# A segment-recurrent attention kernel: the left rows are loaded again one segment earlier, and softmax, copies and small loads change places

## The chip, the cores and the metric

One NeuronCore of a Trainium2 chip runs the whole kernel; the other cores of the chip are not used. The metric is the device time of one execution in microseconds (us), as the median over several runs. The engines are called by the short names of the profile: PE is TensorE, DVE is VectorE, ACT is ScalarE, POOL is GpSimd and SP is SyncE. SP computes nothing here; it issues the large weight transfers.

## The reference: what is computed

The result is `x + A(xn) + B(xn)` for 2048 rows of 1024 numbers, where xn is the layer norm of x.

A is an attention with a memory that is carried from segment to segment. The 2048 rows are cut into 64 segments of 32. In front of each segment stand 8 memory rows, which are the first 8 output rows of the segment before. So each segment depends on the one before it, and the 64 run one after the other:

```python
for s in range(n_seg):
    h = jnp.concatenate([mem, xs], axis=1)              # 8 + 32 rows
    q, k, v = (jnp.einsum('btd,dhe->bhte', h, W) for W in (Wq, Wk, Wv))   # 32 heads of 128
    scores = jnp.where(mask, jnp.einsum('bhqe,bhke->bhqk', q, k) * scale, -1e9)
    o = jnp.einsum('bhqk,bhke->bhqe', softmax(scores), v)
    o = jnp.einsum('bhte,hed->btd', o, Wo)
    mem = o[:, :8, :]
    outs.append(o[:, 8:, :])
```

Wq, Wk, Wv and Wo have 1024 x 4096 numbers each, 32 MB in bf16 together. B picks the two rows with the largest `xn @ w_r`, sends them through a gated feed-forward layer of width 3584 and adds the result to these two rows.

## The kernel before

**The weights.** The four matrices are cut into 64 granules of 512 KB: granules 0 to 47 belong to q, k and v (six phases of eight chunks), 48 to 63 to the output projection. 42 granules stay in on-chip memory for the whole run. The other 22 are streamed again in each segment through six slots of 512 KB (pool `wstream`, tile `g`). `fetch` (L202) issues the next transfer on SP's queue as soon as a slot is free, and a slot is free when PE has used it (`used`, L333). Of three streamed granules one half is held in PSUM (`HELD`) and is copied by ACT (L220), which saves that half of the transfer.

**The rows of a segment.** PE works with 32 rows at a time, the 8 memory rows and the first 24 rows of the segment; the transposed operand is `ST`. The last 8 rows of a segment, its *left* rows, don't feed the next memory, and are therefore computed together for four segments (a group G): 4 x 8 = 32 left rows in `STL`. With j = s % 4, their q is computed in the segment j = 2 of the group before, their k in j = 3, their v in j = 0 of their own group. q and k go through an ACT copy `QS` (L446) and a store to DRAM (`qkl_d`, L450), and each segment loads its own part back as `QKL` (`load_qkl`, L340). The attention outputs of the left rows are gathered in `OTL` over the group, and the output projection of the left rows is done in segment j = 3 and after it, into the PSUM tile `WL`.

**The order.** Nothing is planned by a scheduler: the program is written out in order (`manual_schedule`), and each engine runs its own instructions in the order in which they were emitted. In a segment, six phases (`PHASES`: q, k of the first 16 heads, q, k of the second 16, then v of both) run over eight chunks each (L572 to L616). `hook(p, kc, fn)` puts a function behind chunk kc of phase p; when the place is reached, `fn` emits its instructions for all engines (L598). `ends` is a list of functions that is run when a phase is over (L615). `todo` holds what a segment leaves for the next one's hooks. After the six phases come 16 steps w of the output projection into `WO`, with the last parts of the attention at w = 4 and 8.

**The places that the change touches.**

- `load_left` (L248) loads 4 x 8 left rows by four transfers of 16 KB from POOL's queue into a tile with the tag "vm", of which there is one. The same buffer serves the tiles `VM`, `QS` and `OB` in turn.
- After the last segment of a group, `left_load` at (1,3) of the next segment (j = 0) loads the left rows of the finished group again, `left_norm` at (2,4) normalises them (PE, DVE L259 to L262, POOL L263), and `left_store` at (3,4) adds them to `WL` (`residual`, PE, L302), copies the sum to `OL` (ACT, L688) and stores it by four POOL transfers (L691). Seven of the ten resident granules of WL's projection are worked off in the hooks (0,1) to (1,5) of the same segment. In the last group these three functions run in the tail of the program, L721 to L723.
- `scores(half)` (L464), at (2,5) and (4,5): PE computes q k, DVE finds the maximum and subtracts it (L479, L480), and `softmax(half)` is put into `ends`: ACT's exponential (L484), DVE's sum, reciprocal, two multiplications into `PM` and `PL` and two transposes (L485 to L500), POOL's memset of `PL` for the first half, and last the load of the next segment's QKL (L340).
- `transposes` (L427) and `transposes_left` (L439): when a phase is over, ACT copies `PSm` to `XB` (L602), and one or more chunks later PE transposes it into the single PSUM tile of the tag "t", from where DVE copies it to `QT` or `KT` (L435, L437). The left rows do the same with `XBl` and `QS`.
- `left_keys(half)` (L459), at (0,1) and (3,0): POOL copies the left rows' keys from `QKL` into `KT` (L462), which `scores` needs.

The tags "xb" (two buffers) and "pm" (one buffer) hold `XB`, `XBl`, `PT2` and `OL`, and `XNR` and `PM`, in this order.

Of the kernel before, what the change touches and what calls it, by code (L numbers as in the profile page):

```python
# [8 lines left out]
BF16 = mybir.dt.bfloat16  # L9
# [18 lines left out]
def kernel(  # L28
# [16 lines left out]
    nc = tc.nc  # L45
# [199 lines left out]
        queue.dma_start(out=X[0:4 * XM, :], in_=x2[s * SEG:s * SEG + XM, :].rearrange("r (g c) -> (r g) c", g=4))  # L245
        return X

    def load_left(G, queue=nc.gpsimd):  # L248
        X = one.tile([P, 512], BF16, tag="vm", name="XL")
        for sl in range(4):  # L250
            r0 = (4 * G + sl) * SEG + XM
            queue.dma_start(out=X[32 * sl:32 * sl + 32, 0:256],  # L252
                                in_=x2[r0:r0 + XL, :].rearrange("r (g c) -> (r g) c", g=4))
        return X

# [136 lines left out]
    for s in range(NSEG):  # L392
# [46 lines left out]
        def transposes_left(mat, half, XB, g):  # L439
            PTq = psT.tile([P, 4, 4, 32], BF16, tag="t", name="PTq")  # L440
            for il in range(4):
                nc.tensor.transpose(out=PTq[:, il, :, :].rearrange("p j r -> p (j r)"), in_=XB[:, il * P:(il + 1) * P],
                                    identity=IDENT[:, :])
            QS = one.tile([P, 4, 16, XL], BF16, tag="vm", name="QS") if half == 0 and s > 0 else \
                two.tile([P, 4, 16, XL], BF16, tag="xb", name="QS")
            nc.scalar.copy(out=QS.rearrange("p s h r -> p h s r"),  # L446
                           in_=PTq.rearrange("p i j (s r) -> p (i j) s r", s=4))

            def save():
                nc.gpsimd.dma_start(out=qkl_d[g][mat, half].rearrange("p s c -> p (s c)"),  # L450
                                    in_=QS.rearrange("p s h r -> p (s h r)"))

            if s == 0:
                nc.gpsimd.tensor_copy(out=first_left(half)[:, mat, :].rearrange("p (h r) -> p h r", r=XL), in_=QS[:, 0, :, :])
                save()
            else:
                hook(2 * half + mat + 1, {(0, 0): 5, (1, 0): 4, (0, 1): 7, (1, 1): 4}[mat, half], save)

        def left_keys(half):  # L459
            if s > 0:  # L460
# [3 lines left out]
        def scores(half):  # L464
            q, k = QT[half], KT[half]
            for il in range(4):
                for jq in range(4):
                    hh = 4 * il + jq
                    nc.tensor.matmul(SPS[32 * jq:32 * jq + 32, il, 0, :], lhsT=q[:, hh, :], rhs=k[:, hh, :],
                                     start=(il == 0), stop=True, tile_position=(0, 32 * jq), skip_group_check=True)  # L470
                    nc.tensor.matmul(SPS[32 * jq:32 * jq + XL, il, 1, :], lhsT=QKL[half][:, 0, hh * XL:(hh + 1) * XL],
                                     rhs=k[:, hh, :], start=False, stop=True, tile_position=(0, 32 * jq),
                                     skip_group_check=True)
            nc.tensor.matmul(SPS.rearrange("p i a k -> p i (a k)"), lhsT=IDENT[:, :],  # L474
                             rhs=MASK[:, :].unsqueeze(1).to_broadcast([P, 4, 2 * NK]),
                             start=False, stop=True, skip_group_check=True)
            S8 = SPS.rearrange("p i a k -> p (i a) k")
            NM = one.tile([P, 8], F32, tag="nm", name="NM")
            nc.vector.tensor_reduce(out=NM[:, :], in_=S8, axis=AX.X, op=ALU.max, negate=True)  # L479
            nc.vector.tensor_tensor(out=S8, in0=S8, in1=NM[:, :].unsqueeze(2).to_broadcast([P, 8, NK]), op=ALU.add)  # L480
            ends.append(lambda: softmax(half, S8, NM))

        def softmax(half, S8, DN):
            nc.scalar.activation(out=S8, in_=S8, func=ACTF.Exp, scale=SCALE)  # L484
            nc.vector.tensor_reduce(out=DN[:, :], in_=S8, axis=AX.X, op=ALU.add)  # L485
            nc.vector.reciprocal(out=DN[:, :], in_=DN[:, :])
            PM = one.tile([P, 8, 32], BF16, tag="pm", name="PM")
            PLt = PL.rearrange("p i a k -> p (i a) k")
            if half == 0:
                jp = (j + 3) % 4  # L490
                nc.gpsimd.memset(PLt[:, :, XL * jp:XL * (jp + 1)], 0.0)
            dnb = DN[:, :].unsqueeze(2)
            nc.vector.tensor_tensor(out=PM[:, :, :], in0=S8[:, :, 0:32], in1=dnb.to_broadcast([P, 8, 32]), op=ALU.mult)
            nc.vector.tensor_tensor(out=PLt[:, :, XL * j:XL * (j + 1)], in0=S8[:, :, 32:NK],
                                    in1=dnb.to_broadcast([P, 8, XL]), op=ALU.mult)
            PT2 = one.tile([P, 2, 4, 64], BF16, tag="pt", name="PT2") if half == 0 else \
                two.tile([P, 2, 4, 64], BF16, tag="xb", name="PT2")
            PTm, PTl = PT2[:, 0], PT2[:, 1]
            nc.vector.transpose(out=PTm.rearrange("p i q -> p (i q)"), in_=PM.rearrange("p b k -> p (b k)"))
            nc.vector.transpose(out=PTl.rearrange("p i q -> p (i q)"), in_=PLt.rearrange("p b k -> p (b k)"))  # L500
            PTs[half] = (PTm, PTl)
            if s == 0 and half == 1:
                QKLs.append(load_qkl(1, 0))
                QKLs.append(load_qkl(1, 1))
            elif 0 < s < NSEG - 1:
                QKLs.append(load_qkl(s + 1, half))

        def new_otl():
# [53 lines left out]
        if s == NSEG - 1:  # L562
            hook(0, 6, routed_d)
            hook(2, 2, routed_e)
        hook(2, 5, lambda: scores(0))
        hook(4, 5, lambda: scores(1))
        if j == 0:
            hook(5, 1, new_otl)
        hook(5, 3, lambda: attend(0, 0))
# [2 lines left out]
        for p, (mat, half) in enumerate(PHASES):  # L572
# [27 lines left out]
            if mat < 2:  # L600
                XB = two.tile([P, 512], BF16, tag="xb", name="XB")
                nc.scalar.copy(out=XB[:, :], in_=PSm[:, :])  # L602
                hooks.setdefault((p + 1, (2, 1, 3, 1)[p]), []).insert(0, lambda m=mat, h=half, b=XB: transposes(m, h, b))
                if PSl is not None:
                    XBl = two.tile([P, 512], BF16, tag="xb", name="XBl")
                    (nc.scalar.copy if p == 2 else nc.vector.tensor_copy)(out=XBl[:, :], in_=PSl[:, :])  # L606
                    hooks.setdefault((p + 1, (4, 3, 6, 3)[p]), []).insert(
                        0, lambda m=mat, h=half, b=XBl, g=left[mat]: transposes_left(m, h, b, g))
            else:
                c0 = half * 512  # L610
                if PSl is not None:
                    nc.scalar.copy(out=VL[:, c0:c0 + 512], in_=PSl[:, :])
                VM[half] = one.tile([P, 512], BF16, tag="vm", name="VM")
                nc.scalar.copy(out=VM[half][:, :], in_=PSm[:, :])  # L614
# [29 lines left out]
        for w in range(16):  # L644
            if w == 4:
                attend(1, 0)
            if w == 8:
                attend(1, 1)
            Gv = granule(48 + w)
            project(WO, w, Gv, lhs_main, w == 15)  # L650
            if j == 3:
                if 48 + w in streamed:
                    project(WL, w, Gv, lhs_left, first=not started)
                    started = True
                else:
                    deferred.append((w, Gv))
            used(48 + w)
# [15 lines left out]
        if j == 3:  # L673
            spots = [(0, 1), (0, 3), (0, 5), (0, 7), (1, 1), (1, 3), (1, 5), (1, 7), (2, 1), (2, 3)]
            for pk, (w, Gv) in zip(spots, deferred[3:]):
                todo.append((pk, lambda w=w, Gv=Gv, WL=WL, lhs=lhs_left: project(WL, w, Gv, lhs)))
            end = {}

            def left_load(G=G, end=end):
                end["x"] = load_left(G)  # L680

            def left_norm(G=G, end=end):
                norm_left(G, end["x"])

            def left_store(G=G, WL=WL, end=end):
                residual(WL, end["x"][:, 0:256], P, False)
                OL = two.tile([P, 512], BF16, tag="xb", name="OL")
                nc.scalar.copy(out=OL[:, 0:256], in_=WL[:, 0:256])  # L688
                o4 = out2[4 * G * SEG:4 * (G + 1) * SEG, :].rearrange("(s r) d -> s r d", s=4)
                for g in range(4):  # L690
                    nc.gpsimd.dma_start(out=o4[:, XM:SEG, 256 * g:256 * (g + 1)], in_=OL[32 * g:32 * (g + 1), 0:256])  # L691

            todo += [((1, 3), left_load), ((2, 4), left_norm), ((3, 4), left_store)]
        if s + 1 < NSEG:
            ST = nxt["st"]


    lc.close()
    for pk, fn in todo[:-3]:
        fn()  # L700
    fin = ctx.enter_context(tc.tile_pool(name="fin", bufs=1, reuse_waits="tile"))
    XSP = fin.tile([P, KC, 32], BF16, name="XSP")
# [4 lines left out]
    for w in range(2):  # L707
# [3 lines left out]
        for kc in range(KC):  # L711
            for fh in range(2):
# [6 lines left out]
                                     start=(kc == 0), stop=(kc == KC - 1), tile_position=(0, 32 * q))  # L719
                fetch()  # L720
                n += 1  # L721
                if n in (1, 10, 15):
                    todo[-3 + (1, 10, 15).index(n)][1]()  # L723
    OUTR = fin.tile([2, D], BF16, name="OUTR")
    for c in range(2):
        nc.gpsimd.dma_start(out=OUTR[c:c + 1, :], in_=out2[bass.ds(vals[c], 1), :])
# [68 lines left out]
```

## Time and profile before

Three runs took 2198.06, 2203.74 and 2211.63 us; the median is 2203.74 us. The profiled execution has a span of 2208.3 us.

| engine | busy us | share of the span | instructions |
|---|---|---|---|
| PE | 1764.8 | 80% | 36202 |
| PE weight load | 900.5 | 41% | 36202 |
| DVE | 752.3 | 34% | 2328 |
| ACT | 705.9 | 32% | 1738 |
| POOL | 543.0 | 25% | 1030 |

| queue | packets | MB | share of 16 DMA engines |
|---|---|---|---|
| q1, SP's weights | 267652 | 732.79 | 90.8% |
| q0, POOL's transfers | 23520 | 26.06 | 3.6% |

The profile page gives 768.74 MB in all and a mean of 348 GB/s. How to read what follows: a *wait* is idle time of an engine before an instruction, put down to what came last before the instruction could run. The *chain* goes back from the last instruction of the program, at each step to what released it. The *timeline* gives start, duration, engine, line, operation and names, and in brackets the idle time before it and its releaser. A *window* is a stretch of time with the busy time and the number of instructions of each engine in it. The first segment takes 115.7 us, since it also loads the resident weights and computes the statistics of all rows; the other 63 segments take about 29 to 39 us each; and the tail with the feed-forward layer of B takes the rest.

### The profile page before, as it was taken

The numbers are of one execution on the slowest core, as the hardware profiler recorded it, in microseconds if no ns is written. First come the engines' busy times: TensorE is split into PE (matmuls) and PEld (weight loads), VectorE is DVE, ScalarE is ACT, GpSimd is POOL, SyncE is SP. The second block draws the span as 40 slices with busy tenths as digits, with TensorE's granted clock in tenths as the row PEclk, the third lists the DMA queues.
The fourth block names the chain that finished last, engine by engine and source line by source line (L and its number), as shares of the span: only waits on it lengthen the run. The fifth ranks groups of instructions, "written<-read, shape, count | busy, mean of one in ns | idle before, by whom it ended". The sixth has DMA issues, their size and how long they took to land.

```text
span 2208.3 us, 82817 instructions
## 1 busy us (share of the span) xinstructions
PE 1764.8 (80%) x36202; PEld 900.5 (41%) x36202; DVE 752.3 (34%) x2328; ACT 705.9 (32%) x1738; POOL 543.0 (25%) x1030
## 2 busy tenths in 40 slices
PE   2578788878888888888888788888888878888775
PEld 1234344444434444443444444444444434444341
DVE  5533332333333233333323333332333333233330
ACT  4533233323233333333333233332333323233320
POOL 4322213222121322222122222222222222222111
PEclk8689999999989999999999999998999999899986
DMA  9899999989999999999999999999999999899989
GB/s 358 332 363 365 339 354 331 368 300 346 350 323 371 352 354 347 346 360 330 365 338 384 313 345 377 336 376 318 365 351 348 375 322 367 305 379 352 360 310 347
DMA packets 294351, 768.74 MB, mean 348 GB/s; under 512 B 37458, under 2 KB 42770, under 8 KB 293988
## 3 DMA queue, kind: packets, MB, share of 16 engines
q1 hardware_dynamic: 267652, 732.79, 90.8%
q0 software_dynamic: 23520, 26.06, 3.6%
q8 instruction: 283, 4.64, 0.8%
q10 hardware_dynamic: 2816, 4.59, 0.6%
q14 instruction: 80, 0.66, 0.1%
HBM read 750.68 MB, written 12.59 MB: 346 GB/s over the span
## 4 chain that ended last, share of the span: by engine, by line
PE 42%; DMA 38%; DVE 7%; issue 6%; ACT 4%; POOL 3%; ACTq 0%; DVEq 0%; POOLq 0%; SPq 0%
PE PSm L581 21%; DMA g<-in_A_Wo_dram 13%; DMA g<-in_A_Wq_dram 9%; PE PSl L594 7%; PE OA L632 4%; DMA XL<-in_A_x_dram 4%; DMA qkl_d<-QS 3%; DMA g<-in_A_Wv_dram 2%; PE PTq L430 2%; PE WL L632 2%; DMA XP<-in_A_x_dram 1%; ACT XB L602 1%; POOL XL L252 1%; PE SPS L474 1%; DMA out_dram<-OB 1%
## 5 line engine op out<-in xcount | busy, mean ns | idle before, releaser
L581 PE MATMUL PSm<-wres,ST 128*32 128x512 bf16 x8192 | 774.6, 409 | 20.4 <-DVE ST L309 17.9
L581 PE MATMUL PSm<-g,ST 128*32 128x512 bf16 x4096 | 428.8, 407 | 44.2 <-DMA g<-in_A_Wq_dram 26.9
L581 PEld LDWEIGHTS <-ST 128*32 128x32 bf16 x12288 | 301.7, 99 | 373.7 <-issue 139.9
L632 PEld LDWEIGHTS <-OT 128*32 128x32 bf16 x8192 | 215.4, 97 | 145.3 <-issue 133.9
L220 ACT COPY g<-HELD 128x1024 bf16<-128x1024 bf16 x189 | 191.2, 1012 | 259.4 <-PE PSm L581 169.8
L632 PE MATMUL OA<-wres,OT 128*32 128x256 bf16 x5120 | 235.2, 277 | 26.2 <-issue 20.9
L602 ACT CAST XB<-PSm 128x512 bf16<-128x512 f32 x256 | 149.9, 585 | 317.0 <-PE PSm L581 316.9
L632 PE MATMUL OA<-g,OT 128*32 128x256 bf16 x3072 | 159.0, 278 | 74.0 <-DMA g<-in_A_Wo_dram 70.1
L594 PE MATMUL PSl<-wres,STL 128*32 128x512 bf16 x2048 | 205.9, 404 | 9.0 <-DVE XBl L606 8.3
L340 POOL DMA_DIRECT2D QKL<-qkl_d x126 | 91.9, 729 | 363.9 <-PE SPS L474 175.7
L665 POOL DMA_DIRECT2D out_dram<-OB x256 | 129.5, 513 | 66.2 <-DVE OB L661 35.5
L535 ACT CAST OT<-OA 128x128 bf16<-128x128 f32 x256 | 67.9, 265 | 227.7 <-PE OP L529 226.3
L430 PE MATMUL PTq<-IDENT,XB 128*128 128x128 bf16 x1024 | 106.3, 229 | 43.0 <-ACT XB L602 28.1
L462 POOL COPY KT<-QKL 128x128 bf16<-128x128 bf16 x128 | 38.2, 299 | 375.9 <-PE OA L632 363.1
L479 DVE TENSOR_REDUCE NM<-SPS 128x8 f32<-128x320 f32 x128 | 62.8, 490 | 199.0 <-PE SPS L474 199.0
L430 PEld LDWEIGHTS <-XB 128*128 128x128 bf16 x1024 | 63.2, 100 | 157.1 <-ACT XB L602 115.1
L594 PEld LDWEIGHTS <-STL 128*32 128x32 bf16 x3072 | 87.3, 101 | 91.8 <-issue 35.1
L614 ACT CAST VM<-PSm 128x512 bf16<-128x512 f32 x128 | 77.4, 604 | 140.6 <-PE PSm L581 140.6
L535 DVE CAST OT<-OP 128x128 bf16<-128x128 f32 x128 | 37.3, 291 | 224.4 <-PE OP L529 224.4
L437 DVE COPY KT<-PTq 128x512 bf16<-128x512 bf16 x128 | 54.2, 424 | 164.3 <-PE PTq L430 162.8
L594 PE MATMUL PSl<-g,STL 128*32 128x512 bf16 x1024 | 105.6, 403 | 2.9 <-ACT XBl L606 2.8
L527 PEld LDWEIGHTS <-VM 32*128 32x128 bf16 x2048 | 62.7, 91 | 90.1 <-issue 54.2
(140 smaller groups left out, 2303.2 us busy)
## 6 DMA issues: line engine op xcount, KB each, us to landing
g<-in_A_Wo_dram SPq DMA_DIRECT2D x384, 512.0 KB, 6.7
g<-in_A_Wq_dram SPq DMA_DIRECT2D x321, 512.0 KB, 7.5
g<-in_A_Wk_dram SPq DMA_DIRECT2D x257, 512.0 KB, 6.1
g<-in_A_Wv_dram SPq DMA_DIRECT2D x257, 512.0 KB, 6.9
g<-in_A_Wq_dram SPq DMA_DIRECT2D x63, 256.0 KB, 5.8
g<-in_A_Wk_dram SPq DMA_DIRECT2D x63, 256.0 KB, 5.3
g<-in_A_Wv_dram SPq DMA_DIRECT2D x63, 256.0 KB, 6.3
qkl_d<-QS POOLq DMA_DIRECT2D x64, 128.0 KB, 5.6
```

What stands on the lines that cost most here:

```text
L220: nc.scalar.copy(out=t[:, 1024:2048], in_=held[what[1]][:, :].bitcast(BF16))
L340: nc.gpsimd.dma_start(out=t[:, :, :], in_=qkl_d[s // 4][:, half, :, s % 4, :].rearrange("m p c -> p m c"))
L430: nc.tensor.transpose(out=PTq[:, il, :, :].rearrange("p j r -> p (j r)"), in_=XB[:, il * P:(il + 1) * P], identity=IDENT[:, :])
L479: nc.vector.tensor_reduce(out=NM[:, :], in_=S8, axis=AX.X, op=ALU.max, negate=True)
L527: nc.tensor.matmul(o, lhsT=VM[half][q0:q0 + 32, il * P:(il + 1) * P], rhs=PTm[q0:q0 + 32, il, 0:NK], start=True, stop=False, tile_position ...
L535: copy(out=OT[half][:, 2 * ph + jl, :, :], in_=ov[:, :, 0:SEG])
L581: nc.tensor.matmul(PSm[32 * jq:32 * jq + 32, :], lhsT=ST[:, kc, :], rhs=Gv[:, 512 * jq:512 * (jq + 1)], start=(kc == 0), stop=(kc == KC - ...
L594: nc.tensor.matmul(PSl[32 * jq:32 * jq + 32, :], lhsT=cur["stl"][:, kl, :], rhs=Gl[:, 512 * jq:512 * (jq + 1)], start=(kl == 0), stop=(kl ...
L602: nc.scalar.copy(out=XB[:, :], in_=PSm[:, :])
L614: nc.scalar.copy(out=VM[half][:, :], in_=PSm[:, :])
L632: nc.tensor.matmul(PS[32 * g:32 * g + 32, 0:256], lhsT=lhs(h), rhs=Gv[:, D * hs + 256 * g:D * hs + 256 * (g + 1)], start=(first and hs == ...
L665: nc.gpsimd.dma_start(out=out2[s * SEG:s * SEG + XM, 256 * g:256 * (g + 1)], in_=OB[32 * g:32 * g + XM, 0:256])
```

## The change

It has four parts.

1. The left rows are loaded again not in segment j = 0, but in segment j = 3 of their own group, at w = 8 of the output projection, and into a tile of the tag "xb". Norm and store move up to (0,6) and (1,6). `OL` goes to the tag "pm". It is meant to have the rows on the chip when their norm is due.
2. Only ACT's exponential stays in `ends`. The rest of the softmax of the first half is emitted at (3,4), behind DVE's copy of the second half's q (the transposes at (3,3)), so that this copy doesn't queue behind it.
3. The loads of the next segment's left q and k leave `softmax` and get places of their own, behind the copy of the left keys at (3,0): at (3,5) and (4,7), or both at (4,7) in segments whose left keys are still being saved (j = 3, and the first segment).
4. Most transposes, the scores and the stores of `QS` move one chunk back, so that what they wait for has more time.

The diff, cut to its core:

```diff
-    def load_left(G, queue=nc.gpsimd):
-        X = one.tile([P, 512], BF16, tag="vm", name="XL")
+    def load_left(G, queue=nc.gpsimd, again=False):
+        X = two.tile([P, 512], BF16, tag="xb", name="XL") if again else one.tile([P, 512], BF16, tag="vm", name="XL")
...
-                hook(2 * half + mat + 1, {(0, 0): 5, (1, 0): 4, (0, 1): 7, (1, 1): 4}[mat, half], save)
+                hook(2 * half + mat + 1, {(0, 0): 6, (1, 0): 5, (0, 1): 7, (1, 1): 5}[mat, half], save)
...
-            ends.append(lambda: softmax(half, S8, NM))
+            ends.append(lambda: nc.scalar.activation(out=S8, in_=S8, func=ACTF.Exp, scale=SCALE))
+            rest = lambda: softmax(half, S8, NM)
+            if half == 0:
+                hook(3, 4, rest)
+            else:
+                ends.append(rest)
...
         def softmax(half, S8, DN):
-            nc.scalar.activation(out=S8, in_=S8, func=ACTF.Exp, scale=SCALE)
...
-            if s == 0 and half == 1:
-                QKLs.append(load_qkl(1, 0))
-                QKLs.append(load_qkl(1, 1))
-            elif 0 < s < NSEG - 1:
+
+        def next_left(*halves):
+            for half in halves:
                 QKLs.append(load_qkl(s + 1, half))
...
-        hook(2, 5, lambda: scores(0))
-        hook(4, 5, lambda: scores(1))
+        hook(2, 6, lambda: scores(0))
+        hook(4, 6, lambda: scores(1))
+        if s + 1 < NSEG:
+            if s == 0 or j == 3:
+                hook(4, 7, lambda: next_left(0, 1))
+            else:
+                hook(3, 5, lambda: next_left(0))
+                hook(4, 7, lambda: next_left(1))
...
-                hooks.setdefault((p + 1, (2, 1, 3, 1)[p]), []).insert(0, lambda m=mat, h=half, b=XB: transposes(m, h, b))
+                hooks.setdefault((p + 1, (3, 2, 3, 2)[p]), []).insert(0, lambda m=mat, h=half, b=XB: transposes(m, h, b))
...
-                    hooks.setdefault((p + 1, (4, 3, 6, 3)[p]), []).insert(
+                    hooks.setdefault((p + 1, (5, 4, 6, 4)[p]), []).insert(
...
             if w == 8:
                 attend(1, 1)
+                if j == 3:
+                    XLT = load_left(G, again=True)
...
-            def left_load(G=G, end=end):
-                end["x"] = load_left(G)
...
-                residual(WL, end["x"][:, 0:256], P, False)
-                OL = two.tile([P, 512], BF16, tag="xb", name="OL")
-                nc.scalar.copy(out=OL[:, 0:256], in_=WL[:, 0:256])
+                residual(WL, X[:, 0:256], P, False)
+                OL = one.tile([P, 256], BF16, tag="pm", name="OL")
+                nc.scalar.copy(out=OL[:, :], in_=WL[:, 0:256])
...
-            todo += [((1, 3), left_load), ((2, 4), left_norm), ((3, 4), left_store)]
+            todo += [((0, 6), left_norm), ((1, 6), left_store)]
...
-                if n in (1, 10, 15):
-                    todo[-3 + (1, 10, 15).index(n)][1]()
+                if n in (6, 14):
+                    todo[-2 + (6, 14).index(n)][1]()
```

## Prediction

> **What bounds the kernel now.** I read the page first, then the busy windows cut at the ends of the ACT copies of OB (L660), so that one window is one segment, then PE's waits, then the timeline around the longest one.
>
> ```profile
> DMA  9899999989999999999999999999999999899989
> PE 42%; DMA 38%; DVE 7%; issue 6%; ACT 4%; POOL 3%; ACTq 0%; DVEq 0%; POOLq 0%; SPq 0%
> ```
>
> The DMA engines are nearly always busy with weights that are streamed again for every segment, and the chain that ended last is split between PE and DMA. So PE and the stream run neck and neck: a PE wait costs time only where it leaves all six stream slots full and the DMA engines without work. Which segments do that, the windows tell (second number: length; last three: granted clock, DMA share, GB/s; packets overlap, so a share can pass 1):
>
> ```profile
> core 0: us, PE busy (x) PEld busy (x) DVE busy (x) ACT busy (x) POOL busy (x), PEclk, DMA share, GB/s
> 1501.86:1536.35 34.49, 29.02 (x620) 15.30 (x612) 10.61 (x35) 10.77 (x27) 10.43 (x21) 0.88 0.86 285
> 1536.35:1567.74 31.39, 24.58 (x481) 11.55 (x481) 11.22 (x36) 9.31 (x24) 8.12 (x17) 0.95 1.02 378
> 1567.74:1599.63 31.89, 26.73 (x547) 13.55 (x547) 10.41 (x32) 10.88 (x27) 6.58 (x14) 0.95 0.96 351
> 1599.63:1631.34 31.71, 27.25 (x607) 15.20 (x611) 11.20 (x33) 10.39 (x27) 6.47 (x14) 0.97 1.01 383
> ...
> 467.85:506.27 38.42, 28.47 (x612) 14.98 (x604) 10.62 (x35) 10.77 (x28) 10.45 (x21) 0.87 0.80 271
> 730.98:763.68 32.70, 27.80 (x615) 15.04 (x605) 10.62 (x35) 10.85 (x27) 10.37 (x21) 0.95 0.95 326
> 1631.34:1662.86 31.52, 26.92 (x623) 14.82 (x613) 10.62 (x35) 10.77 (x28) 10.42 (x21) 0.97 0.95 315
> ```
>
> The first four are segments 44 to 47, j = 0 to 3. Over segments 4 to 63 the means are 35.1, 30.7, 31.6 and 31.9 us. Only j = 0 leaves DMA idle for long (share 0.86). The last three are other j = 0 segments: 38.4 us where PE's wait for the left rows is 7.6 us, 32.7 and 31.5 us where it is nothing and 1.1 us.
>
> ```profile
> PE WL L302 <- POOL XL L263: 47.4, 14, 7.6
> PE PTq L430 <- ACT XB L602: 28.1, 51, 7.4
> PE SPS L469 <- POOL KT L462: 25.7, 16, 4.3
> PE PTq L442 <- DVE QT L435: 24.9, 16, 1.7
> PE PS L277 <- DVE QT L435: 14.2, 15, 1.3
> ```
>
> The first belongs to j = 0, the last three almost wholly to j = 3, 2 and 1. They are the waits that this change aims at.
>
> ```profile
> 1495.11 0.71 POOL L340 DMA_DIRECT2D QKL<-qkl_d  x1 [6.27 <-DMA qkl_d<-QS]
> ...
> 1508.64 2.01 POOL L252 DMA_DIRECT2D XL<-in_A_x_dram  x4 [1.79 <-DMA out_dram<-OB]
> ...
> 1516.80 0.29 DVE L261 TENSOR_SCALAR XL<-XL,SC 128x256 bf16<-128x256 bf16 x1 [4.88 <-DMA XL<-in_A_x_dram]
> ...
> 1517.50 0.66 POOL L263 TENSOR_TENSOR XL<-XL 128x256 bf16<-128x256 bf16 x1 [6.85 <-DVE XL L262]
> ...
> 1518.21 0.41 PE L302 MATMUL WL<-XL,IDENT 128*32 128x256 bf16 x4 [3.81 <-POOL XL L263]
> 1518.38 0.66 PE L581 MATMUL PSm<-wres,ST 128*32 128x512 bf16 x4
> ```
>
> The chain of the j = 0 wait: the store of OB frees tile "vm" (1508.6), four loads of XL are issued, they land, DVE normalises, POOL adds, PE adds the residual at (3,4) (phase, chunk). PE stands for 3.81 us. After that a group of four matmuls takes 0.66 us instead of 0.39:
>
> ```profile
> 1518.40:1523.40 5.00, 4.49 (x44) 1.72 (x40) 2.66 (x8) 1.27 (x3) 3.23 (x6) 0.50 0.74 236
> ```
>
> **What the Trainium skill says.** "TensorE: Matmul & The Clock Gate", What's actually happening: the array falls to half clock after an idle window of about 3.4 us and needs about as long of work to rise. The trace agrees: clock 0.50 for 5 us behind a wait of 3.81 us, so the wait costs more PE time than its length. "Perfetto Trace Analysis", Identifying the Most-Contended Engine: matmul occupancy is a poor measure of distance to the limit; here PE is 80% busy and weight loads 41%, and it is the DMA share of a segment that separates 35 us from 31. "DMA: Bandwidth & Descriptors", Two DMAs through the same engine are not ordered: only the completion semaphore, waited for by the issuer, orders a read behind a write; that is POOL's 6.27 us in front of L340, with the copy of left keys (L462) queued behind it whenever it comes later in POOL's order. The same page, Anatomy of one DMA, would give 2.0 us for 16 KB; the trace has 5.3 us (XL, median), and I use that.
>
> **The change part by part.** No instruction and no byte is added or taken away (PE has as many rows in both); only order, buffers and waits change.
>
> 1. Left rows. The load goes from (1,3) of j = 0 to w = 8 of the output projection of the segment before, into "xb"; norm to (0,6), residual to (1,6). Is it there in time? In the trace above the save of the left keys that POOL must outwait begins at 1488.3 and lands after 6.3 us (other segments 4.8 to 6.0). Then follow two QKL loads (0.73 each), X (0.55), four XL issues (2.0) and 5.3 us of landing from the last: 1494.6 + 1.5 + 0.55 + 1.5 + 5.3 = 1503.4. (0,6) was reached at 1506.0; without the 1.0 us key wait of j = 3, some 1505. Over 15 segments the margin worked out in this way runs from about -0.7 to +5 us. From the norm PE needs 0.29 + 0.28 + 0.66, about 1.3 us, and (1,6) comes 3.4 us after (0,6), so 2 us more are free. The wait of 47.4 us goes.
>
> What is that worth? Of 15 j = 0 segments, the five with the shortest such wait (mean 0.9 us) last 33.2 us, the five longest (mean 4.9) 36.9: 0.92 us per us. Together with the j = 1 segment behind, which can catch up, 64.7 against 67.4: 0.67. A line through all, with PE's waits put down to "issue" beside it, has a slope of 0.85 for the pair. 47.4 x 0.85 = 40 us; the ends are 32 and 44.
>
> 2. Behind that wait DVE is late too: PE then waits 0.7 us in each j = 0 segment for q's copy (L435). It goes with it: 15 x 0.7 x about 0.4 = 4 us (0 to 9).
>
> 3. The new home of OL is "pm", which the first half's softmax writes (PM). A new wait: PM's write for the landing of four OL stores. Residual at about 1509.7, copy 0.37, four issues of 0.59, landing 4.4 (longest 6.1) from the last: 1516.4 (1518.1). PM would be ready at about 1515.3, so DVE stands for 1.1 (2.8) us. Behind PM stand PL, two transposes and the copy of KT: 1.2 + 0.4 us, so KT is there at 1518.0 (1519.7); SPS, which scores(1) overwrites, is free with PL, a microsecond earlier. PE, from (3,4) at 1514.4, does three chunks of 0.22, two of 0.22, then five of 0.43 with the left rows' matmuls, and a transpose group of 0.3: scores(1) at about 1518.0. So 0 to 1.7 us of PE wait; I take 0.3: 15 x 0.3 x 0.85 = +4 us (0 to +22).
>
> 4. Softmax of the first half behind q's copy, QKL loads behind the key copy, transposes one chunk later. They take away the last three lines of the waits, 65 us in all. But the DMA engines did not notice: in the 6 us from the beginning of each such wait their idle time is nothing on average (-0.17, -0.12, -0.09 us; packets overlap), against 2.6 us in the 12 us after an L302 wait. PE catches up from full slots. Hidden by the stream: -3 us (0 to -20). The transposes waiting for ACT's XB are the same case, but for the first segment, whose order of statistics shifts a little: 0, plus or minus 3.
>
> 5. The tail: its waits in PE are for streamed weights (8.5 and 8.4 us), so moving norm and store there is nothing.
>
> Sum: 2203.7 - 40 - 4 + 4 - 3 = 2160.7; I say 2160.
>
> **The rivals.** A, the forecast, 2145 to 2175: 0.62. B, all waits count: besides the 44 us of the steep slope, the 65 us of part 4 move PE ahead in j = 1 to 3, at a third, and part 2 in full: 2203.7 - 44 - 22 - 9 = 2129. For it speak the shares of 0.96 in j = 2; against it those above 1 elsewhere. 0.13. C, a wait takes the place: XL lands late or the OL stores hold PM, and 2 us per j = 0 segment stay: 2203.7 - 1.16 x 15 x 0.85 - 7 = 2182. For it the margins below zero in three segments; against it the 2 us behind them. 0.19. D, slower: both together, 5 us in each j = 0 segment where 3.2 were: + 1.8 x 0.85 x 15 = 2227. Against it, both chains would have to take over 3 us more than measured. 0.06.
>
> **How the numbers follow.** Time 2160, from A. Range 2130 to 2187: it takes in A, nearly all of B and the better half of C. 1% is 22 us, so faster needs below 2181.7: A, B and half of C, 0.84; within 1%: the rest of C and a little of D, 0.11; slower 0.05.
>
> **What would show it.** Right: the wait of WL (L302) for XL gone; j = 0 segments at 31.5 to 33 us with a share near 0.93 and clock near 0.95; j = 1 to 3 within 0.5 us of before, though their three waits are gone. Part 3: a DVE wait in front of PM for out_dram<-OL of about 1 us, a PE wait for KT under 0.5. Wrong: a wait of L302 or L469 over 2 us in j = 0, or j = 1 to 3 shorter by over 1 us each.

## The result

The changed kernel takes 2136.47 us (median of 4 runs, 2127.16 to 2143.36), the kernel before 2207.34 us beside it: ratio 0.968 with a 95% interval of 0.963 to 0.973, some 71 us less. On a second chip it was 2126 us against 2206 (ratio 0.9636). Forecast were 2160 us and a range of 2130 to 2187: direction and range hold (the second chip's 2126 us lies just below the range), but of 71 us only 44 were forecast. The profiled execution of the changed kernel has a span of 2125.5 us, that of the kernel before 2208.3; it is one of the faster runs, so the times per segment below add up to a little more than the medians.

The page of the changed kernel, the same two lines as before (DMA share in 40 slices, and the chain that ended last by engine):

```profile
DMA  9899999999999999999999999999999999999998
DMA 50%; PE 41%; DVE 3%; issue 3%; ACT 3%; POOL 0%; ACTq 0%; DVEq 0%; SPq 0%; POOLq 0%
```

The chain has moved from PE and its helpers to the transfers: DMA 38% before, 50% now, and DVE and POOL together 10% before, 3% now. The windows of segments 44 to 47 (j = 0 to 3), then two more j = 0 segments (20 and 40); the second number is the length, the last three are clock, DMA share and GB/s:

```profile
1439.19:1470.80 31.61, 26.80 (x612) 14.06 (x604) 10.55 (x35) 10.71 (x27) 8.43 (x17) 1.00 0.96 332
1470.80:1501.62 30.82, 23.58 (x481) 11.65 (x481) 11.05 (x36) 9.50 (x24) 8.05 (x17) 1.00 1.01 378
1501.62:1533.45 31.83, 27.65 (x547) 13.36 (x547) 10.43 (x32) 10.97 (x27) 6.53 (x14) 0.95 0.95 352
1533.45:1563.47 30.02, 27.29 (x616) 15.16 (x619) 11.01 (x33) 10.67 (x26) 8.46 (x18) 1.00 1.02 388
699.19:730.30 31.11, 26.45 (x615) 14.10 (x605) 10.52 (x35) 10.70 (x27) 8.42 (x17) 1.00 0.98 341
1313.62:1347.74 34.12, 27.84 (x615) 14.60 (x613) 10.62 (x35) 10.70 (x27) 8.41 (x17) 0.95 0.91 319
```

Segment 44 was 34.49 us at clock 0.88 and 285 GB/s. Over segments 4 to 63 the windows give:

| j | length before, us | after | GB/s before | after | clock before | after |
|---|---|---|---|---|---|---|
| 0 | 35.10 | 31.70 | 297 | 333 | 0.91 | 0.99 |
| 1 | 30.68 | 30.68 | 380 | 377 | 0.95 | 0.95 |
| 2 | 31.58 | 30.94 | 356 | 366 | 0.96 | 0.98 |
| 3 | 31.94 | 30.54 | 363 | 376 | 0.95 | 0.99 |

15 segments of each kind: 51 us from j = 0, nothing from j = 1, 10 from j = 2 and 21 from j = 3 are 82 us, the difference of the two spans. PE's waits, of which the five shown before were the aim:

```profile
PE OA L641 <- DMA g<-in_A_Wo_dram: 89.4, 147, 2.5
PE PSm L590 <- DMA g<-in_A_Wv_dram: 53.1, 81, 2.6
...
PE SPS L469 <- DVE KT L437: 13.8, 13, 2.1
...
PE PTq L442 <- DVE QT L435: 5.6, 2, 4.3
...
PE PTq L430 <- ACT XB L611: 5.0, 21, 1.1
```

The wait of WL for XL (47.4 us) is gone from the list, the one of scores for the left keys and the two for q's copy nearly so. PE now waits for weights instead. One wait is new and was not among the large ones before: scores for KT, 13.8 us. Its cause is in DVE's waits and in the timeline of segment 44:

```profile
DVE PM L497 <- DMA out_dram<-OL: 59.8, 15, 4.6
```

```profile
1434.20 1.98 POOL L252 DMA_DIRECT2D XL<-in_A_x_dram  x4
...
1444.69 0.29 DVE L261 TENSOR_SCALAR XL<-XL,SC 128x256 bf16<-128x256 bf16 x1
...
1445.38 0.67 POOL L263 TENSOR_TENSOR XL<-XL 128x256 bf16<-128x256 bf16 x1 [1.83 <-DVE XL L262]
...
1448.58 2.43 POOL L698 DMA_DIRECT2D out_dram<-OL  x4 [2.54 <-ACT OL L695]
...
1456.97 0.42 DVE L497 TENSOR_TENSOR PM<-SPS,NM 128x256 bf16<-128x256 f32 x1 [3.66 <-DMA out_dram<-OL]
...
1458.13 0.38 DVE L437 COPY KT<-PTq 128x512 bf16<-128x512 bf16 x1
...
1458.57 0.21 PE L469 MATMUL SPS<-KT,QT 128*32 128x40 bf16 x4 [0.76 <-DVE KT L437]
```

The upper half is what part 1 was for: XL is issued 10 us ahead of its norm, and neither DVE nor PE waits for it here. The lower half is its price: OL's stores land at 1456.9, PM waits 3.66 us for them, the copy of KT is behind PM, and PE waits 0.76 us for KT.

### The profile page after: what moved, and what is told of

The parts are those of the page before. It is cut to its first block, busy times and chain, and to the rows that moved or that the text cites. A ratio compares the mean times of both kernels' runs of the same rounds, so it can differ in the third digit from the quotient of the medians.

```text
span 2125.5 us, 82723 instructions
## 1 busy us (share of the span) xinstructions
PE 1732.3 (82%) x36202; PEld 883.3 (42%) x36202; DVE 746.4 (35%) x2328; ACT 713.0 (34%) x1738; POOL 540.6 (25%) x1030
## 4 chain that ended last, share of the span: by engine, by line
DMA 50%; PE 41%; DVE 3%; issue 3%; ACT 3%; POOL 0%; ACTq 0%; DVEq 0%; SPq 0%; POOLq 0%
DMA g<-in_A_Wo_dram 21%; PE PSm L590 21%; DMA g<-in_A_Wv_dram 11%; DMA g<-in_A_Wq_dram 7%; PE PSl L603 6%; PE OA L641 4%; DMA out_dram<-OL 4%; DMA g<-in_A_Wk_dram 2%; PE WL L641 2%; PE PTq L430 2%; DMA wres<-in_A_Wo_dram 1%; DMA g<-in_B_w_up_dram 1%; PE SPS L474 1%; DMA g<-in_B_w_gate_dram 1%; PE PTq L442 1%
## 5 line engine op out<-in xcount | busy, mean ns | idle before, releaser
L590 PE MATMUL PSm<-wres,ST 128*32 128x512 bf16 x8192 | 757.0, 394 | 19.7 <-DVE ST L309 17.9
L590 PE MATMUL PSm<-g,ST 128*32 128x512 bf16 x4096 | 415.8, 395 | 98.4 <-DMA g<-in_A_Wv_dram 53.1
L590 PEld LDWEIGHTS <-ST 128*32 128x32 bf16 x12288 | 294.3, 97 | 429.8 <-issue 198.8
L603 PE MATMUL PSl<-wres,STL 128*32 128x512 bf16 x2048 | 199.9, 391 | 14.0 <-DVE XBl L615 13.4
L450 POOL DMA_DIRECT2D qkl_d<-QS x64 | 36.6, 572 | 278.4 <-ACT QS L446 278.4
```

Source lines behind the costliest of these rows:

```text
L590: nc.tensor.matmul(PSm[32 * jq:32 * jq + 32, :], lhsT=ST[:, kc, :], rhs=Gv[:, 512 * jq:512 * (jq + 1)], start=(kc == 0), stop=(kc == KC - ...
L603: nc.tensor.matmul(PSl[32 * jq:32 * jq + 32, :], lhsT=cur["stl"][:, kl, :], rhs=Gl[:, 512 * jq:512 * (jq + 1)], start=(kl == 0), stop=(kl ...
```

## The experiments

Two theories stood against each other. Theory 1 is the prediction's: only the wait of j = 0 is visible, since the DMA engines were busy around all others. Theory 2: the short waits of the other segments cost time too.

**The change cut in two.** Four kernels ran beside each other. The yardstick:

> The changed kernel as it is, as a yardstick on the same chip for the three runs beside it. Both theories expect the ratio already measured, 0.968 of the kernel before, some 70 us less.

Measured: 2126.2 us against 2206.3, ratio 0.9636 (0.9598 to 0.9673), 80 us less.

Part 1 alone (the load at w = 8), with OL in a place that nobody else waits for:

```diff
+                if j == 3:
+                    XLT = load_left(G, again=True)
...
-                OL = two.tile([P, 512], BF16, tag="xb", name="OL")
-                nc.scalar.copy(out=OL[:, 0:256], in_=WL[:, 0:256])
+                OL = OB[:, 256:512]
+                nc.scalar.copy(out=OL, in_=WL[:, 0:256])
...
-            todo += [((1, 3), left_load), ((2, 4), left_norm), ((3, 4), left_store)]
+            todo += [((0, 6), left_norm), ((1, 6), left_store)]
```

> The kernel before with part 1 alone: left rows loaded again at w = 8 of segment j = 3, norm at (0,6), store at (1,6). So that no other part is needed, OL lies in the unused half of the tile OB and not in the tag pm, which the first half's softmax would wait for. Theory 1 (the prediction: only the 3.2 us wait of j = 0 is visible, the other waits are hidden by the stream) expects nearly the whole gain, 62 to 70 us, with j = 2 and j = 3 a little shorter because something in j = 0 carries over. Theory 2 (the short waits of j = 2 and 3 cost time too) expects 45 to 52 us, j = 0 at 31.5 to 32 us and j = 2 and 3 unchanged at 31.6 and 31.9 us.

Measured: 2136.9 us, ratio 0.9688 (0.9644 to 0.9732), 69 us less. The windows give j = 0 at 31.20 us, 3.9 us less than before, j = 1 at 29.63 (30.68 before), j = 2 at 31.50 and j = 3 at 31.53 us. PE's waits keep what the other parts are for:

```profile
PE PTq L442 <- DVE QT L435: 29.6, 17, 4.6
...
PE SPS L469 <- POOL KT L462: 23.3, 16, 4.5
```

All but part 1:

```diff
-            todo += [((0, 6), left_norm), ((1, 6), left_store)]
+            todo += [((1, 3), left_load), ((2, 4), left_norm), ((3, 4), left_store)]
```

> The changed kernel without part 1: left rows loaded, normalised and stored at the old places of segment j = 0; parts 2 to 4 stay. Theory 1 expects 0 to 8 us less than the kernel before, the 65 us of short PE waits being gone for nothing. Theory 2 expects 20 to 31 us less, with j = 3 near 30.5 and j = 2 near 30.9 us and j = 0 still near 35 us.

Measured: 2171.6 us, ratio 0.9844 (0.9806 to 0.9882), 35 us less. j = 3 lasts 29.94 us, 2.0 less than before, j = 2 31.31; j = 0 is still at 34.85, and its wait is even longer:

```profile
PE WL L302 <- POOL XL L263: 63.5, 14, 7.1
```

So theory 1 hits one number and misses the other: part 1 alone gives 69 us, within its 62 to 70, but the rest of the change is worth 35 us by itself and not 0 to 8. Theory 2 misses both: 69 us and not 45 to 52, 35 us and not 20 to 31. Not all of the 69 us is sure to be part 1's: in that run's profile j = 0 gives 58 us, and j = 1, which holds none of part 1's instructions, another 16. In the runs of this document that put nothing into j = 1 it lasts between 29.6 and 30.9 us; the cause of this was not looked for.

**The new wait.** The changed kernel with OL moved:

```diff
-                OL = one.tile([P, 256], BF16, tag="pm", name="OL")
+                OL = OB[:, 256:512]
```

> The changed kernel with OL in the unused half of OB in place of the tag pm. It takes away the new wait of the first half's PM for the four OL stores, and with it PE's wait for KT in j = 0 (SPS L469 for KT L437, 0.80 us a segment). If j = 0 is still bound by PE there, 15 x 0.80 x 0.85 = 10 us less than the changed kernel; if the stream hides it, 0 to 3 us less.

Measured: 2115.0 us, ratio 0.9561 (0.9516 to 0.9606): 11 us under the changed kernel by the medians, 17 by the ratios. DVE's wait for OL's stores is gone, PE's wait for KT falls from 12.2 us in the yardstick run to 3.5, and j = 0 from 31.63 to 30.71 us. The wait that took a place was real, and its price is about its length: 0.8 us in each of 15 segments, 12 us.

With OL beside OB the four corners fit together: before 2206, part 1 alone -69, the rest alone -35, both -91. Part 1 is worth 57 to 69 us and the rest 22 to 35, depending on which comes first.

Part 1 alone exactly as the change has it, with OL in "pm", but the softmax of the first half still at the end of phase 2:

> The kernel before with part 1 alone exactly as the change has it, OL in the tag pm, but the first half's softmax still at the end of phase 2. PM is then due about 4.5 us after the residual of (1,6) and OL's stores land about 7.8 us after it, so DVE stands for some 3 us, q's copy stands behind it and PE waits some 2 us in each j = 0 segment. Expected: 15 x 2 = 30 us more than part 1 with OL beside OB (2137 us), about 2167 us. If the wait is hidden: about 2137 us.

Measured: 2216.5 us against 2213.8, ratio 1.0015 (0.9984 to 1.0046). No gain is left at all: 30 us more than with OL beside OB were expected, and 72 (by the ratios) to 80 came. The new wait is as long as the one removed (PE's waits):

```profile
PE PTq L430 <- DVE QT L435: 48.4, 17, 4.1
```

47.4 us of waiting for XL have turned into 48.4 us of waiting for q's copy, which stands behind PM on DVE. In the changed kernel part 2 puts q's copy ahead of PM. That this is what makes OL in "pm" bearable is read from this line; part 2 was not taken out with OL in "pm", and parts 3 and 4 are missing here too.

**The rest cut into its parts**, each put back in the kernel with OL beside OB (2115 us). The order of the key copy first:

```diff
-                hook(3, 5, lambda: next_left(0))
+                hook(*((2, 7) if j == 3 else (3, 5)), lambda: next_left(0))
```

and the second half's load stays at (4,7) in all segments but the first.

> The kernel with OL beside OB, and one thing put back: in segments j = 3 the first half's QKL load goes ahead of the copy of left keys again, at (2,7), the second half's stays at (4,7). The wait of scores for the left keys (SPS L469 for POOL KT L462, 1.4 us a segment before) should come back. Theory 1 (hidden by the stream, since no DMA idle time follows it): 0 to 4 us over the 2115 us of that kernel. Theory 2 (in j = 3 PE itself hardly waits for weights, 0.4 us a segment before, so what PE loses there is lost): 15 x 1.4 to 2.0 = 20 to 30 us over it.

Measured: 2164.9 us, ratio 0.9829 (0.9768 to 0.9889), 50 us more by the medians and 59 by the ratios. The wait came back in another place than named, and longer:

```profile
PE PTq L442 <- DVE KT L437: 56.7, 16, 4.5
```

```profile
DVE PT L504 <- POOL PL L495: 53.3, 15, 4.3
```

The memset of PL now stands behind the load on POOL, DVE waits for the memset, and PE for DVE. That is 3.5 us in each j = 3 segment where 1.4 were before, so this run does not undo part 3 cleanly, and its 50 to 59 us are not the price of part 3. But it says what a us of waiting costs in j = 3: for 56.7 us of waits, 50 to 59 us of time. In the profile j = 3 lasts 33.30 us against 30.53 and the j = 0 behind it 31.85 against 30.71. PE's waits for weights in j = 3 fall from 1.2 to 0.3 us, so a little was hidden; and PE's busy time grows from 27.4 to 28.0 us at a clock of 0.93 and not 0.975, which is part of the cost.

Then the softmax of the first half (part 2) and the places of transposes, scores and saves (part 4):

```diff
-            if half == 0:
-                hook(3, 4, rest)
-            else:
-                ends.append(rest)
+            ends.append(rest)
```

> The kernel with OL beside OB, and part 2 put back: the first half's softmax runs whole at the end of phase 2, ahead of q's copy on DVE. The waits for q's copy in j = 1 (0.9 us) and j = 2 (1.5 us) should come back. Theory 1: 0 to 4 us over the 2115 us. Theory 2 says that only what exceeds PE's own waits for weights costs: these are 4.0 us in j = 1 and 1.9 us in j = 2 before, so j = 1 stays and j = 2 gets some 0.3 us longer: 3 to 10 us.

Measured: 2117.4 us, ratio 0.9613 (0.9563 to 0.9663). That is 2 us more by the medians, 11 by the ratios, and the intervals overlap. The waits did come back:

```profile
PE PTq L442 <- DVE QT L435: 24.9, 15, 1.7
...
PE PS L277 <- DVE QT L435: 18.3, 15, 1.5
```

43 us of waits in j = 1 and 2, and no cost that is clear of the spread. In exchange PE waits less for weights, by 1.0 us in a j = 1 segment (4.3 to 3.4) and by 1.4 in j = 2 (3.3 to 1.9): this is how such a wait is hidden. In the profile j = 0 is 0.8 us longer, j = 2 0.4 longer and j = 1 1.0 shorter, so single segments move by as much as the effect that is sought.

```diff
-        hook(2, 6, lambda: scores(0))
-        hook(4, 6, lambda: scores(1))
+        hook(2, 5, lambda: scores(0))
+        hook(4, 5, lambda: scores(1))
...
-                hooks.setdefault((p + 1, (3, 2, 3, 2)[p]), []).insert(0, lambda m=mat, h=half, b=XB: transposes(m, h, b))
+                hooks.setdefault((p + 1, (2, 1, 3, 1)[p]), []).insert(0, lambda m=mat, h=half, b=XB: transposes(m, h, b))
```

(and in the same way for the left rows' transposes and the saves)

> The kernel with OL beside OB, and part 4 put back: transposes, scores and the saves of QS one chunk earlier, as before. PE's wait for ACT's XB (0.3 to 0.4 us in j = 0 to 2) should come back. Both theories expect 0 to 6 us over the 2115 us.

Measured: 2105.7 us, ratio 0.9538 (0.9490 to 0.9587). Part 4 is worth nothing that could be measured; the kernel without it, and with OL beside OB, is the fastest median of all, though its interval overlaps with the one beside it. Both beat the changed kernel.

**Is it the clock behind the wait?** Extra matmuls keep PE busy while it would stand for XL in the kernel before:

```diff
+                for _ in range(12 if G + 1 < NT else 0):
+                    for hs in range(2):
+                        for g in range(4):
+                            nc.tensor.matmul(WL[32 * g:32 * g + 32, 256:512], lhsT=IDENT[:, 32 * g:32 * g + 32],
+                                             rhs=res_tiles[57][:, 0:256], start=False, stop=True,
+                                             tile_position=(0, 32 * g), skip_group_check=True)
                 residual(WL, end["x"][:, 0:256], P, False)
```

> The kernel before, with 96 extra matmuls (about 2.6 us of PE work) ahead of the residual at (3,4) of j = 0, written to an unused half of WL, so that PE works while it would stand waiting for the left rows. The wait itself and its length stay; only the array has no idle window. If half of the gain in j = 0 was the clock behind the wait (0.50 for 5 us), j = 0 gets a clock of 0.96 or more and the kernel gets 10 to 25 us faster, although 2.6 us are wasted where the wait is shorter (together some 9 us). If the clock does not matter, it gets 5 to 10 us slower.

Measured: 2204.6 us against 2204.9, ratio 0.9988 (0.9963 to 1.0013). Neither the 10 to 25 us faster nor the 5 to 10 us slower came. The timeline of segment 44 shows that the clock did stay up:

```profile
1486.62 2.79 PE L689 MATMUL WL<-wres,IDENT 128*32 128x256 bf16 x96
1489.24 0.28 PE L302 MATMUL WL<-XL,IDENT 128*32 128x256 bf16 x4
1489.35 0.39 PE L581 MATMUL PSm<-wres,ST 128*32 128x512 bf16 x4
```

Behind the residual a group takes 0.39 us and not 0.66, and the clock of j = 0 is 0.97 on average (0.91 before). The busy times of the 15 j = 0 segments from the fifth segment on, in the kernel before, with part 1 alone, and with the filler:

```profile
sum 526.55, PE 428.97 PEld 227.76 DVE 159.26 ACT 161.60 POOL 156.36; mean PE 28.60 PEld 15.18 DVE 10.62 ACT 10.77 POOL 10.42
sum 467.93, PE 405.67 PEld 219.52 DVE 160.09 ACT 159.87 POOL 127.82; mean PE 27.04 PEld 14.63 DVE 10.67 ACT 10.66 POOL 8.52
sum 531.43, PE 448.64 PEld 259.40 DVE 159.40 ACT 162.00 POOL 156.49; mean PE 29.91 PEld 17.29 DVE 10.63 ACT 10.80 POOL 10.43
```

The filler is 2.9 us of the last 29.91; without it PE is busy for 27.0 us, as with part 1 alone. So the half clock costs 1.6 us of PE time in a j = 0 segment. But with the filler j = 0 lasts 35.43 us, against 35.10, in a profile that is the fastest of its 22 runs (2184.6 us). Filler and rest of the wait are 0.6 us longer than the wait of before, idle time put down to "issue" grows by 0.65 us, and PE's waits for weights and for q's copy by 0.5. What was saved is spent again on these, so this run does not tell what the half clock alone costs the kernel.

**An added delay**, 2.6 us of useless matmuls at (5,0) in one kind of segment (j = 0 in the diff, 1 and 3 in the two others), in the kernel with OL beside OB:

```diff
+        if s >= 4 and j == 0:
+            def fill():
+                FT = psT.tile([P, 256], F32, tag="t", name="FT")
+                for n in range(24):
+                    for g in range(4):
+                        nc.tensor.matmul(FT[32 * g:32 * g + 32, :], lhsT=IDENT[:, 32 * g:32 * g + 32],
+                                         rhs=res_tiles[57][:, 0:256], start=(n == 0), stop=(n == 23),
+                                         tile_position=(0, 32 * g), skip_group_check=True)
+            hook(5, 0, fill)
```

> The kernel with OL beside OB, and 2.6 us of useless PE work (96 matmuls of 256 columns into a free PSUM tile) at (5,0) of each segment j = 0 from the fifth on: a delay of known length that leaves the clock alone. PE waits 1.7 us for weights in such a segment. Theory 1 (one us of delay costs 0.85 us): +33 us over the 2115 us. Theory 2 (PE's own waits for weights are the slack, the rest costs one for one): between 15 x 0.9 and 15 x 2.6, +14 to +39 us.

> The same 2.6 us of useless PE work at (5,0) of each segment j = 1, where PE waits 4.3 us for weights. Both theories expect nothing, 0 to 5 us over the 2115 us.

> The same 2.6 us of useless PE work at (5,0) of each segment j = 3, where PE waits 1.2 us for weights and the DMA engines have no idle time. Theory 1 (no DMA idle time, so hidden): 0 to 5 us over the 2115 us. Theory 2: 15 x 1.4 to 2.6, +21 to +39 us.

The kernel before took 2213.8 us beside these, so I compare ratios; a difference of two of them is uncertain by about 0.006 to 0.007, or 13 to 15 us.

| 2.6 us of matmuls in 15 segments (39 us) | us | ratio | over 0.9561 | the segment itself in the profile, us longer |
|---|---|---|---|---|
| j = 0 | 2157.5 | 0.9752 | 0.0191, 42 us | 3.4 |
| j = 1 | 2136.9 | 0.9681 | 0.0120, 26 us | 0.8 |
| j = 3 | 2148.6 | 0.9734 | 0.0173, 38 us | 2.8 |

The delay came out longer than 2.6 us: PE's idle time put down to "issue" grows too, by 0.4 us in a j = 0 segment, 1.3 in j = 1 and 1.4 in j = 3. In exchange PE waits less for weights: not at all less in j = 0 (1.7 us in both), 2.3 us and not 4.3 in j = 1, 0.1 and not 1.2 in j = 3. So in j = 0 the delay is paid in full, which both theories allow within the uncertainty. In j = 3 some two thirds of it are paid; theory 1's 0 to 5 us fall, and theory 2's 21 to 39 hold. In j = 1 about half of it goes into shorter waits for weights, but it is not free, as both theories had it: GB/s fall from 377 to 356 in the profile. So PE's own waits for weights hide a delay, but not up to their full length.

## Why the prediction was right, and where its sizes were wrong

The items are those of the prediction's list, not the parts of the change.

**Item 1, the wait of j = 0: right in mechanism, too small.** XL was on the chip 0.2 to 5.2 us ahead of its norm in the 15 segments, where -0.7 to +5 had been worked out, and the wait went. The term that was mis-sized is the slope of 0.85, with ends of 0.67 and 0.92. With part 1 alone j = 0 gets 3.9 us shorter, where PE's waits for XL and for q's copy behind it, 3.16 + 0.72 = 3.9 us, are gone: a slope of about 1, so 47 us for the 47.4 and not 40. The pair's slope let the j = 1 segment behind catch up a part of the wait; but j = 1 lasts 30.68 us in the kernel before and in the changed one. The slope was read from segments that differ by themselves, and of the five with the shortest wait three had other losses (2.5 to 2.7 us put down to "issue"), which made them long without the wait and the slope flat. The line with "issue" beside it had given 1.12 for j = 0 alone; taking the pair's 0.85 in its place was the choice that failed. The delay added in j = 0 agrees with 1, but its uncertainty takes in 0.85 as well. Part 1 alone measured 69 us, 57 when it came second.

**The clock.** The prediction said that the wait costs more PE time than its length, after the Trainium skill, "TensorE: Matmul & The Clock Gate", What's actually happening. The trace does show the half clock for 5 us, and of the 3.9 us that j = 0 gets shorter with part 1 alone 1.6 are PE's busy time (28.6 to 27.0 us) and only 2.3 are idle time, since PE then waits 1.1 us more for weights. So the price of the wait comes up to its length through the faster matmuls. But the kernel with the clock kept up by a filler is no faster (0.9963 to 1.0013), and whether a kept-up clock would pay without the filler's own cost was not tried.

**Item 2, DVE's lateness behind the wait: right in kind, undersized.** The 0.7 us per segment had been counted at a factor of 0.4. It is gone with part 1. Both together, 3.9 us x 15 = 58 us, are what the 15 j = 0 segments lose in the profile of part 1 alone, and lie at the lower end of the 57 to 69 measured for part 1.

**Item 3, OL in "pm": foreseen, but three to four times too short.** The DVE wait is 59.8 / 15 = 4.0 us and not 1.1 (at most 2.8), PE's wait for KT 0.8 us and not 0.3, the cost 11 us (17 by ratios) and not 4. Two terms of the sum were off. POOL issued the first store 1.05 us after the start of the residual (1447.53 to 1448.58 in segment 44) where 0.55 was counted; and the stores took 6.7 us to land (5.1 to 7.9) and not 4.4. The landing time was from the trace, but from another moment: behind PE's long wait, where in segment 44 the DMA engines moved 160 GB/s while the stores landed; in the changed kernel they moved 289.

**Item 4, "hidden by the stream": wrong.** -3 us were taken and 0 to -20 allowed; all but part 1 measured -35, and -22 by the medians (-28 by the ratios) where part 1 is there already. The step that failed is the one from "the DMA engines did not notice" to "hidden". The reading itself stands: in the 6 us from the beginning of the waits for the left keys the DMA engines moved 385 GB/s on average, more than the 380 of a whole j = 1 segment. But a busy stream right behind a wait does not hide the wait. It is hidden where PE would have waited for weights later on anyway. In the kernel before that was 4.0 us in a j = 1 segment, 1.9 in j = 2 and only 0.4 in j = 3, so 1.4 us of waiting for the left keys in j = 3 had next to nothing to be hidden in; and 1.4 us is what j = 3 gained in the profile. The GB/s of a whole segment are a weaker sign. j = 3 moved 363 against 380 in j = 1, which is 4.5% of 31.9 us, 1.4 us; but the same working with j = 2's 356 gives 2.0 us, and j = 2 gained 0.6. For the waits for q's copy the judgement holds as far as can be measured (2 to 11 us, not clear of nothing), and for part 4's shifted places as well. So the gain beyond j = 0 is, by elimination, mainly the order of loads and key copy in j = 3; no run undoes that order cleanly.

**Item 5 and the first segment** hold: the first segment lasts 115.7 us in both, the tail 59.6 and 61.5 us.

In sum: 44 us were forecast. At a price of 1 the terms are 58 for j = 0, about 30 for j = 3 and j = 2, and 11 to be paid for OL, about 77; measured were 71 and 80. The 30 and the 11 are taken from the runs, so this shows that the terms are complete and not that they could have been known. The range held because it took in nearly all of rival B, and because OL's price, too low by 7 us, made up for a part of the gains that were too low by some 40. Rival B, which let the short waits count, was right in kind; its third of 65 us was 22, at the lower end of 22 to 35. Of the signs named, j = 0 at 31.7 us and j = 1 unchanged came true, the clock even higher (0.99). j = 2 and j = 3, 0.6 and 1.4 us shorter, left the 0.5 us that were allowed, and the two waits of item 3 were longer than their signs. The sign for a wrong step, over 1 us shorter, came in j = 3 alone and pointed to item 4.

What stays open: how much of a delay in j = 1, where PE waits for weights for longest, is really paid (26 us by the ratios, uncertain by 13 to 15, and 12 by the length of the j = 1 segments), and why 2.3 us of waits for weights stay beside it; why j = 1 moves by a us from run to run; and why part 1 gives 69 us when it comes first and 57 when it comes last, a difference that is within the intervals.

## What to carry to other kernels

Where a weight stream and PE run neck and neck, judge whether a PE wait is hidden by how long PE itself waits for weights in that stage, not by a DMA share near 1 and not by a busy stream right behind the wait; best add a delay there and see, and read from the trace how long the delay really was. A buffer that is freed by a store is a wait for that store to land, at the speed that transfers have in that stage: give it to a tag whose next writer comes late, here 11 us for one line. And parts of a change can carry each other: the early left rows with OL in "pm" brought nothing while the rest of the change was missing.

## What the runs showed of the hardware that was not expected

- Half clock on PE for 5 us behind a long wait costs 1.6 us of PE's busy time in a j = 0 segment (28.6 against 27.0 us), but a filler that kept the array busy brought only the clock of j = 0 from 0.91 to 0.97 and left the time as it was, 2204.9 and 2204.6 us: its own delay and the waits behind it took the gain.
- Small stores from POOL land later here where the stream is denser: four stores of 16 KB each took 4.4 us (median) at the old place and 6.7 us at the new one in the changed kernel; while they landed in segment 44, the DMA engines moved 160 and 289 GB/s. With OL at the old place and the rest changed it was 4.1 us.
- The DMA share of a window can reach 1.02 to 1.03 (packets overlap), and 0.99 was still 17 GB/s below the fastest stage.
